# An FFT-and-experts kernel: the flag before the branch, the first rows of the redo in the branch, idle matmuls in two waits, and scatters without an order

## The chip, the cores and the metric

The kernel runs on one core of a Trainium2 chip. The metric is the device time of one execution in microseconds (us). The engines are named as in the profile: PE is TensorE, with PEld its weight loads, DVE is VectorE, ACT is ScalarE, POOL is GpSimd and SP is SyncE. A q behind an engine's name (PEldq, SPq, POOLq) is its sequencer: loads of a register, branches, waits and DMA issues.

## What is computed

Three layers stand one behind the other, on 8 sequences of 3072 tokens with 256 channels (24576 tokens): a spectral mixing, a first expert layer of hidden width 2048 that all tokens share, and a second layer of 8 experts with 768 places each, of which a token uses one.

```python
    X = np.fft.rfft(x, axis=1)
    Xr, Xi = (X.real.astype(np.float32), X.imag.astype(np.float32))
    Yr = Xr @ w_r - Xi @ w_i + b_r
    Yi = Xr @ w_i + Xi @ w_r + b_i
    lam = 0.01
    Yr = np.sign(Yr) * np.maximum(np.abs(Yr) - lam, 0.0)
    Yi = np.sign(Yi) * np.maximum(np.abs(Yi) - lam, 0.0)
    Y = Yr.astype(np.float64) + 1j * Yi.astype(np.float64)
    y = np.fft.irfft(Y, n=x.shape[1], axis=1)
...
    h = np.maximum(x @ w_in, 0.0)
    return (h * h @ w_out).astype(np.float32)
...
    logits = x @ w_gate
    expert_idx = np.argmax(logits, axis=1)
...
    for i in range(N):
        e = expert_idx[i]
        if counts[e] < capacity:
            disp[e, counts[e]] = x[i]
            pos[i] = counts[e]
            counts[e] += 1
            keep[i] = True
    h = np.maximum(np.einsum('ecd,edf->ecf', disp, w1), 0.0)
    y = np.einsum('ecf,efd->ecd', h, w2)
    out = np.zeros((N, D), dtype=np.float32)
    for i in range(N):
        if keep[i]:
            out[i] = gate_w[i] * y[expert_idx[i], pos[i]]
```

The 8 experts have 6144 places for 24576 tokens. Once all places are taken, no later token changes the output.

## The kernel before

**Main loop.** The tokens are worked in 48 blocks of 512 (NBLK, BLK), six to a sequence (BPB). The hidden width of the first expert layer is cut into 16 f steps (KF). In each f step `l1` makes one piece of the hidden layer, and steps of the spectral stage of a later sequence (`mix_a`, `mix_b`, `sa` and others, one after the other from a list) run in between. The last step of `mix_b` ends in four additions on POOL (L362, the tile y).

Blocks 0 to 10 are full: `l2` makes their output rows, which are scattered to `disp`, the experts' places. All later blocks are late: only the logits of the gate are made (`l2_gate`, bf16, into acc[0]), and the input rows of those tokens that got a place are scattered to a list `late` in DRAM, for the output to be made afterwards (redo). `route` holds the routing of a block as a list of small operations, of which the loop runs up to five in each f step of the next block: the prefix sums of the counts (`places`, giving pos), ok, kf and kp (which tokens stay), the place numbers, cnt (the counts so far), the ranks in the late list (`ranks`, lp, lx, li), the scatter to `late` in four parts (up to MV = 4 per f step), then mn (the smallest count), flag (1 if any expert has room), lcnt and nlate (the length of the list).

From block 12 on (NSURE), each late block has a check at f step 9 (FX): what is left of the routing is run, one spectral step if one is halfway, and all engines load flag (L1132) and go on only if it is 1 (L1133). The nest of conditions is closed behind the loop (L1165): an engine that finds 0 branches to the end, and there waits for what the others and the DMA queues still have open. The loop was left at the 20th check, in block 31.

**Redo.** Behind the loop, four last gate matmuls run (acc[0], L580). Then all engines load nlate (L1216), SP loads the first 256 rows of `late` (`redo_load`, into a tile of the ring zt) and the first expert's weights (`m2_loadw`), TensorE transposes the rows (`redo_y`, L1210), and chunks of 256 rows follow, each under a condition on nlate: `l1` and, three steps behind, `l2` (L565, matmuls of WO = 264 columns: 256 channels and 8 logits, of which the redo does not use the logits). Six chunks run. Their rows are scattered to `disp`.

**Second expert layer.** For each of 8 experts: the rows of `disp` are loaded (zd, L1262), transposed (L1294), and multiplied (L1327, L1351, both f32r) in six tiles of 128 rows. DVE writes yo (L1360) and POOL scatters it to the output rows of its tokens (L1361), 48 scatters in all. Each of them waits for the one before to land, since both write to `out`.

What sets the order: the order in which the program is written is each engine's queue, and the tile framework puts in the waits between engines and DMA queues.

Of the kernel before, what the change touches and what calls it, by code (L numbers as in the profile page):

```python
# [8 lines left out]
F32 = mybir.dt.float32  # L9
# [18 lines left out]
def fft_mix__moe__moe2_kernel(  # L28
# [40 lines left out]
    FX = 9  # L69
# [21 lines left out]
    PER_F = 5  # L91
    assert 3 * E <= CG and KF % 4 == 0
# [467 lines left out]
    def l2(acc, f, q, tiles=TPB):  # L560
        sh, sl = q[f]
        for t in range(tiles):
            n = 0
            for a, m in ((sh, 0), (sh, 1), (sl, 0)):
                nc.tensor.matmul(  # L565
                    acc[t][:, 0:WO],
                    a[:, t * P:(t + 1) * P],
                    wo_s[:, m, f, :],
                    start=(f == 0 and n == 0),
                    stop=(f == KF - 1 and n == 2),  # L570
                )
                n += 1
# [92 lines left out]
    def route(i, zt, lg, lt):  # L665
# [53 lines left out]
        if lt is not None:  # L719
            kf = small([TPB], F32, "kf")  # L720
            op(v.tensor_reduce, kf, ok, axis=AX.X, op=ALU.add)
            op(v.tensor_copy, kp5[:, 0:TPB], kf)
        op(v.tensor_tensor, u, pos[:, 0:TPB, :], be(ebase), op=ALU.add)
# [3 lines left out]
        op(v.tensor_copy, cnt, pos[:, TPB, :])  # L727
        last = [
            lambda: v.tensor_reduce(mn, cnt, axis=AX.X, op=ALU.min),
            lambda: v.tensor_scalar(flag, mn, float(cap), None, op0=ALU.is_lt),  # L730
        ]
        if lt is not None:
# [8 lines left out]
            ops += [None, ranks]  # L741
# [64 lines left out]
    def setup_c():  # L806
# [17 lines left out]
        nc.gpsimd.iota(tid, pattern=[[P, TPB]], base=0, channel_multiplier=1)  # L824

# [96 lines left out]
    with tc.manual_schedule():  # L922
# [120 lines left out]
        W.li = Ring("li", [P, TPB], I32, 2, lb)  # L1043
        wk_es = ExitStack()
# [16 lines left out]
        cond = ExitStack()  # L1061
        for i in range(NBLK):
# [21 lines left out]
            for f in range(KF):  # L1084
# [40 lines left out]
                if f == FX and i >= NSURE:  # L1125
                    while moves or rops:
                        step = (moves or rops).pop(0)
                        if step is not None:
                            step()
                    if pair[0]:  # L1130
                        fft(1)
                    rv = nc.values_load(flag[0:1, 0:1], min_val=0, max_val=1)  # L1132
                    cond.enter_context(tc.If(rv > 0))  # L1133
# [19 lines left out]
        cond.enter_context(tc.If(rv > 0))  # L1153
# [11 lines left out]
        cond.close()  # L1165
# [20 lines left out]
        if NBLK > NFULL:  # L1186
# [7 lines left out]
            def redo_load(c):  # L1194
                rows = W.zt()
                nc.sync.dma_start(
                    out=rows[:, 0:RT, :],
                    in_=late[c * RB:(c + 1) * RB, :].rearrange("(t p) d -> p t d", p=P),
                )
                return rows  # L1200
# [14 lines left out]

            nv = nc.values_load(nlate[0:1, 0:1], min_val=0, max_val=NREDO * RB)  # L1216
            nxt = redo_load(0)
            w_t[0] = m2_loadw(0)
            y_nxt = redo_y(nxt)
            for c in range(NREDO):  # L1220
                cond.enter_context(tc.If(nv > c * RB))
                rows, y = nxt, y_nxt
                q = []
                for f in range(KF):
# [6 lines left out]
                    if f >= RLAG:  # L1231
                        l2(acc, f - RLAG, q, RT)
                for f in range(KF - RLAG, KF):
                    l2(acc, f, q, RT)
                evac_z(acc, rows, RT)
                scatter(disp, NSLOT, lambda t: rows[:, t, D + 2:D + 3], rows, tiles=RT)
            cond.close()
# [66 lines left out]
        w_t[1] = m2_loadw(1)  # L1304
        for step in m2_split(0, nc.vector) + m2_tr(0):
            step()
        for e in range(E):
# [37 lines left out]
            for t in range(CT):  # L1345
# [15 lines left out]
                nc.gpsimd.indirect_dma_start(  # L1361
# [8 lines left out]
                )  # L1370
# [70 lines left out]
```

## Time and profile before

| what | us |
|---|---|
| median of 3 runs | 2146.16 (2144.68 to 2149.83) |
| span of the profiled execution, first to last instruction | 2143.0 |
| TensorE busy in it | 2058.0 (96%) |
| DVE, ACT, POOL busy | 1389.7, 1121.7, 763.8 |
| leaving the loop, last gate matmul to first transpose of the redo | 1675.4 to 1688.5 |
| redo to first transpose of the second expert layer | 1832.5 to 1842.6 |
| last tile of the output to the end | 2129.7 to 2143.0 |

The profile is of one execution; its time beside the span is not listed, and the span lies 3.2 us below the median. Times of a row count from the span's start. In a timeline a row is: start, duration, engine, line, operation, output <- inputs, shape, count, and in brackets the idle time of that engine before it and what ended it. The columns of a view by source line are engine, operation, inputs and count, then the shortest, median and longest duration in ns, then the first and last start in us.

### The profile page before, as it was taken

How to read it: one execution, taken by the hardware profiler on the slowest of the kernel's cores; microseconds unless marked ns; L12 is line 12 of the kernel's file. 1: busy time of each engine (PE TensorE's matmuls, PEld its weight loads, DVE VectorE, ACT ScalarE, POOL GpSimd, SP SyncE). 2: the span in 40 equal slices, each digit the busy share in tenths (PEclk: the TensorE clock that was granted, in tenths of full speed). 3: DMA queues.
4: the chain of work that ended last, by engine and by line, in shares of the span. 5: the costliest groups of instructions: out<-in, count | busy, mean ns of one | idle time of the engine just before them, and what ended most of it. 6: DMA issues, size and time to landing. Idle time of an engine off the chain costs nothing. (4 is left out here: it accounts for less than half of the span.)

```text
span 2143.0 us, 35810 instructions
## 1 busy us (share of the span) xinstructions
PE 2058.0 (96%) x13307; PEld 1756.3 (82%) x13307; DVE 1389.7 (65%) x2814; ACT 1121.7 (52%) x2227; POOL 763.8 (36%) x728
## 2 busy tenths in 40 slices
PE   6899999999999999999999999999999799799997
PEld 3878999989999987777677776777777699799997
DVE  3855666644666665888868886688858566434332
ACT  4644444454454445666656666566656455433331
POOL 2641222110222222566426554365625210244441
PEclk8978999999999999999999999999999899899999
DMA  9758665134111115221242213411152100523300
GB/s 272 227 172 302 197 211 178 55 104 119 50 43 46 41 43 157 61 60 57 84 128 58 61 37 114 121 52 56 39 159 73 58 27 25 172 93 116 97 21 25
DMA packets 163080, 214.89 MB, mean 100 GB/s; under 512 B 14622, under 2 KB 136020, under 8 KB 162882
## 3 DMA queue, kind: packets, MB, share of 16 engines
q1 hardware_dynamic: 145538, 167.94, 26.4%
q0 software_dynamic: 10848, 21.63, 3.1%
q10 hardware_dynamic: 6496, 22.81, 3.1%
q8 instruction: 109, 1.79, 0.4%
q14 instruction: 89, 0.73, 0.1%
HBM read 117.95 MB, written 104.43 MB: 104 GB/s over the span
## 5 line engine op out<-in xcount | busy, mean ns | idle before, releaser
L528 PE MATMUL ph<-yh,wi_s 128*128 128x512 f32 (+1 forms) x1780 | 512.2, 410 | 3.9 <-ACT yh L514 2.8
L362 POOL TENSOR_TENSOR y<-tt,cc 64x256 f32<-64x256 f32 x256 | 247.3, 966 | 503.1 <-DVE cc L357 421.8
L528 PEld LDWEIGHTS ph<-yh,wi_s 128*128 128x128 f32 x1780 | 309.1, 189 | 95.4 <-issue 43.3
L565 PE MATMUL acc<-wo_s,sh 128*128 128x264 f32 x1792 | 339.4, 286 | 0.0
L556 DVE TENSOR_TENSOR s<-s 128x512 f32<-128x512 f32 (+1 forms) x272 | 168.5, 619 | 230.6 <-ACT sh L555 230.5
L565 PEld LDWEIGHTS acc<-wo_s,sh 128*128 128x128 f32 x1792 | 287.0, 188 | 13.9 <-issue 1.0
L545 POOL TENSOR_TENSOR ld<-ld 128x512 bf16<-128x512 f32 x164 | 179.5, 1098 | 320.6 <-DVE ld L544 210.9
L544 DVE TENSOR_TENSOR ld<-ls 128x512 f32<-128x512 f32 x329 | 261.2, 798 | 46.4 <-ACT ls L541 44.0
L528 PE MATMUL ph<-yl,wi_s 128*128 128x512 f32 (+1 forms) x890 | 270.7, 385 | 0.2
L565 PE MATMUL acc<-wo_s,sl 128*128 128x264 f32 x896 | 254.7, 284 | 0.2 <-DVE sl L557 0.2
L552 ACT ACTIVATE s<-ph 128x512 f32<-128x512 f32 (+1 forms) x224 | 123.1, 550 | 247.5 <-PE ph L528 246.9
L541 ACT ACTIVATE ls<-ls 128x512 f32<-128x512 f32 x330 | 208.6, 632 | 10.4
L540 ACT ACTIVATE ls<-ph 128x512 f32<-128x512 f32 x221 | 131.3, 594 | 152.2 <-PE ph L528 148.8
L528 PEld LDWEIGHTS ph<-yl,wi_s 128*128 128x128 f32 x890 | 163.2, 189 | 35.1 <-DVE yl L517 1.5
L557 DVE TENSOR_TENSOR sl<-s,sh 128x512 fp32r<-128x512 f32 (+1 forms) x272 | 173.4, 638 | 19.9 <-PE px L247 0.5
L565 PEld LDWEIGHTS acc<-wo_s,sl 128*128 128x128 f32 x896 | 168.5, 188 | 0.5 <-DVE sl L557 0.4
L528 PE MATMUL acc<-yh,wi_s 128*128 128x512 f32 (+1 forms) x628 | 164.7, 384 | 0.5 <-ACT yh L514 0.4
L555 ACT ACTIVATE sh<-s 128x512 fp32r<-128x512 f32 (+1 forms) x272 | 151.4, 557 | 8.6
L545 DVE TENSOR_TENSOR ld<-ld 128x512 bf16<-128x512 f32 x165 | 149.5, 906 | 5.7
L1336 ACT ACTIVATE rh<-pg 128x384 fp32r<-128x384 f32 x128 | 62.7, 490 | 168.0 <-PE pg L1327 166.4
L1351 PE MATMUL po<-w2s,rh 128*128 128x256 f32 x768 | 139.1, 284 | 0.0
L1327 PE MATMUL pg<-xh,w1s 128*128 128x384 f32 x512 | 138.3, 342 | 0.0
(290 smaller groups left out, 3820.4 us busy)
## 6 DMA issues: line engine op xcount, KB each, us to landing
out_dram<-zero SPq DMA_DIRECT2D x48, 512.0 KB, 4.8
u<-ue ACTq DMA_DIRECT2D x53, 384.0 KB, 4.2
uj<-u SPq DMA_DIRECT2D x77, 256.0 KB, 4.0
z<-zj SPq DMA_DIRECT2D x74, 256.0 KB, 2.2
xc<-in_x_dram SPq DMA_DIRECT2D x48, 384.0 KB, 5.3
xc<-z SPq DMA_DIRECT2D x48, 384.0 KB, 3.8
m<-table SPq DMA_DIRECT2D x77, 128.0 KB, 3.1
ma<-table SPq DMA_DIRECT2D x77, 128.0 KB, 4.0
```

The lines of the kernel that those rows point to most:

```text
L362: y_eng[n == r].tensor_tensor(y[64 * r:64 * r + 64, :], t[src, r, :], c[src, r, :], op=ALU.subtract)
L528: nc.tensor.matmul(p, wi_s[:, l, k, f * P:(f + 1) * P], y[:, k, 0:n_tok], start=(n == 0), stop=(n == 5),)
L540: nc.scalar.activation(s, p, AF.Relu)
L541: nc.scalar.activation(s, s, AF.Square)
L544: nc.vector.tensor_tensor(d, s, top(s), op=ALU.subtract)
L545: (gp if f in E_POOL else ve).tensor_tensor(e, d, top(d), op=ALU.subtract)
L555: nc.scalar.activation(sh, s, AF.Square)
L556: nc.vector.tensor_tensor(s, s, s, op=ALU.mult)
L557: nc.vector.tensor_tensor(sl, s, sh.bitcast(F32), op=ALU.subtract)
L565: nc.tensor.matmul(acc[t][:, 0:WO], a[:, t * P:(t + 1) * P], wo_s[:, m, f, :], start=(f == 0 and n == 0), stop=(f == KF - 1 and n == 2),)
L1327: nc.tensor.matmul(p[:, 0:gs], w1s[:, l, k, f * P:(f + 1) * P], y[:, k, g * gs:(g + 1) * gs], start=(n == 0), stop=(n == 5),)
L1351: nc.tensor.matmul(acc, a[:, t * P:(t + 1) * P], w2s[:, m, f, :], start=(n == 0), stop=(n == 3 * KD - 1),)
```

## The change

- The flag is made right behind kf and kp, ahead of the place numbers, and the check stands at f step 8 and not at 9. The break between two f steps ahead of `ranks` is gone, and lcnt and nlate are now the last of the list.
- Each condition gets an else branch (`leave`): there TensorE runs 16 matmuls (WARM) of the identity with 256 columns of zeros into acc[3], which nobody reads, and SP loads the first 256 rows of `late` into a tile of their own (row0). The same load stands at the end of the innermost condition. Behind the join, the first rows are transposed ahead of the load of nlate and of the weights.
- The redo's `l2` is 256 columns wide.
- Behind the redo, TensorE runs 16 such matmuls again.
- All output scatters are declared to be free of an order among themselves (a token has one place at most).

```diff
-    FX = 9
+    FX = 8
+    WARM = 16
...
-    def l2(acc, f, q, tiles=TPB):
+    def l2(acc, f, q, tiles=TPB, width=WO):
...
-                    acc[t][:, 0:WO],
+                    acc[t][:, 0:width],
                     a[:, t * P:(t + 1) * P],
-                    wo_s[:, m, f, :],
+                    wo_s[:, m, f, 0:width],
...
             op(v.tensor_copy, kp5[:, 0:TPB], kf)
+        op(v.tensor_copy, cnt, pos[:, TPB, :])
+        op(v.tensor_reduce, mn, cnt, axis=AX.X, op=ALU.min)
+        op(v.tensor_scalar, flag, mn, float(cap), None, op0=ALU.is_lt)
         op(v.tensor_tensor, u, pos[:, 0:TPB, :], be(ebase), op=ALU.add)
...
-        op(v.tensor_copy, cnt, pos[:, TPB, :])
-        last = [
-            lambda: v.tensor_reduce(mn, cnt, axis=AX.X, op=ALU.min),
-            lambda: v.tensor_scalar(flag, mn, float(cap), None, op0=ALU.is_lt),
-        ]
+        last = []
...
-            ops += [None, ranks]
+            ops.append(ranks)
...
+    def late_rows(c, rows):
+        nc.sync.dma_start(
+            out=rows[:, 0:RB // P, :],
+            in_=late[c * RB:(c + 1) * RB, :].rearrange("(t p) d -> p t d", p=P),
+        )
...
+        row0 = lb.tile([P, RB // P, DW], F32, name="row0")
...
-        cond = ExitStack()
+        ifs = []
+
+        def go_on(value):
+            guard = tc.If(value)
+            ifs.append((guard, guard.__enter__()))
+
+        def warm(p):
+            for _ in range(WARM):
+                nc.tensor.matmul(p[:, 0:D], idt, zero)
+
+        def close_ifs(other=None):
+            while ifs:
+                guard, here = ifs.pop()
+                guard.__exit__(None, None, None)
+                if other:
+                    with here.Else():
+                        other()
+
+        def leave():
+            warm(acc[3])
+            late_rows(0, row0)
...
-        cond.close()
+        late_rows(0, row0)
+        close_ifs(leave)
         if carry:
             l2_gate(acc, KF - 4, carry, first=8)
...
+            nxt = row0
+            y_nxt = redo_y(nxt)
             nv = nc.values_load(nlate[0:1, 0:1], min_val=0, max_val=NREDO * RB)
-            nxt = redo_load(0)
             w_t[0] = m2_loadw(0)
-            y_nxt = redo_y(nxt)
             for c in range(NREDO):
...
-                        l2(acc, f - RLAG, q, RT)
+                        l2(acc, f - RLAG, q, RT, D)
                 for f in range(KF - RLAG, KF):
-                    l2(acc, f, q, RT)
+                    l2(acc, f, q, RT, D)
...
-            cond.close()
+            close_ifs()
+            warm(acc[3])
...
+        sent = []
...
-                nc.gpsimd.indirect_dma_start(
+                inst = nc.gpsimd.indirect_dma_start(
...
-                )
+                ).ins
+                for prev in sent:
+                    tc.declare_no_dep(inst, prev, reason="every token has one slot at most")
+                sent.append(inst)
```

What stands in the engines' queues shows two places. A number behind a name (ld_8208) tells one buffer from another; what an instruction waits for stands in brackets (DMASW and DMAHW are lanes of DMA queues).

First, DVE in the routing of block 30, which runs in block 31 ahead of the 20th check. Before, from cnt to nlate:

```order
L671 COPY cnt<-pos 128x8
L544 TENSOR_TENSOR ld_8208<-ls_8202 128x512 [waits PE_49,Activation_49]
L545 TENSOR_TENSOR ld_8208<-ld_8208 128x512 [waits DVE_49]
L739 TENSOR_SCALAR lp<-acc_1537,lcnt 128x5 [waits PE_49]
L671 SCALAR_TENSOR_TENSOR lx<-lp,kp_91 128x4 [waits DVE_49]
L671 TENSOR_SCALAR li_1551<-lx 128x4 [waits DVE_49]
L729 TENSOR_REDUCE mn<-cnt 128x1
L544 TENSOR_TENSOR ld_8209<-ls_8203 128x512 [waits Activation_49,Pool_49]
L545 TENSOR_TENSOR ld_8209<-ld_8209 128x512 [waits DVE_49]
L730 TENSOR_SCALAR flag<-mn 128x1 [waits DVE_sequencer_49,PE_sequencer_49,SP_sequencer_49,Activation_sequencer_49,Pool_sequencer_49]
L747 COPY lcnt<-lp 128x1
L748 CAST nlate<-lp 128x1
```

And after, from pos on:

```order
L706 TENSOR_TENSOR pos<-px,cnt 128x40 [waits PE_49]
L672 SCALAR_TENSOR_TENSOR ok<-pos,oh_90 128x32 [waits DVE_49]
L672 TENSOR_REDUCE kf<-ok 128x4 [waits DVE_49]
L672 CAST kp_91<-kf 128x4 [waits DVE_49]
L672 COPY cnt<-pos 128x8
L545 TENSOR_TENSOR ld_8208<-ls_8202 128x512 [waits Activation_49]
L672 TENSOR_REDUCE mn<-cnt 128x1 [waits DVE_49]
L672 TENSOR_SCALAR flag<-mn 128x1 [waits PE_sequencer_49,DVE_sequencer_49,Activation_sequencer_49,SP_sequencer_49,Pool_sequencer_49,DVE_49]
L672 TENSOR_TENSOR rv<-pos,ebase 128x32
L672 TENSOR_TENSOR rv<-rv,ok 128x32 [waits DVE_49]
L672 TENSOR_REDUCE sf<-rv 128x4 [waits DVE_49]
L545 TENSOR_TENSOR ld_8209<-ls_8203 128x512 [waits PE_49,Activation_49]
```

The three operations on cnt, mn and flag now stand right behind kp, ahead of rv (the place numbers) and of lp, lx and li (the ranks), which follow further down.

Second, the way out of the loop. SP's queue before, from the join on:

```order
L1216 TENSOR_LOAD nlate [waits DVE_49]
L1216 ISA x2
L1196 DMA zt_1546<-late 128x2x259 [waits DMASW6_49,DMASW5_49,DMASW7_49,DMASW1_49,DMAHW0_49,DVE_49,Activation_49]
L1181 DMA yT<-in_moe_w_dram 128x2x1024 [waits DMAHW1_49,PE_49]
L1182 DMA yT<-in_moe_w_dram 128x8x256 [waits DMAHW2_49,PE_49,Activation_49]
L1237 COMPARE_AND_BRANCH
```

After, with one of the else branches (up to its UNCONDITIONAL_BRANCH) and then the join:

```order
L827 DMA row_1552<-late 128x2x259 [waits DMAHW6_49,DMASW5_49]
L1081 UNCONDITIONAL_BRANCH [waits SP_sequencer_49,DMAHW0_49,DMAHW1_49,DMAHW2_49,DMAHW3_49,DMAHW4_49,DMAHW5_49,DMAHW7_49]
L1244 TENSOR_LOAD nlate [waits DVE_49]
L1244 ISA x2
L1210 DMA yT<-in_moe_w_dram 128x2x1024 [waits DVE_49,DMAHW1_49,PE_49,Activation_49]
L1211 DMA yT<-in_moe_w_dram 128x8x256 [waits DVE_49,DMAHW2_49,PE_49,Activation_49]
L1081 COMPARE_AND_BRANCH
```

The load of the first rows stands in the branch and waits for two lanes; before, it stood behind the join and behind the load of nlate and waited for seven sources.

TensorE's queue at the same place before, from the last gate matmul on:

```order
L580 LDWEIGHTS wgate
L580 MATMUL acc_1535<-ld_8209,wgate 32x512
L1216 TENSOR_LOAD nlate [waits DVE_49]
L1210 MATMUL px<-idt,zt_1546 128x128 [waits DMAHW0_49,DVE_49,PE_49]
L1210 MATMUL px<-idt,zt_1546 128x128
L1210 MATMUL px<-idt,zt_1546 128x128 [waits DVE_49,PE_49]
L1210 MATMUL px<-idt,zt_1546 128x128
L1237 COMPARE_AND_BRANCH
```

And after, behind the join and the first of the four gate matmuls (the 16 added matmuls stand in the else branches, each of which ends in a jump to the join):

```order
L581 LDWEIGHTS wgate
L581 MATMUL acc_1535<-ls_8204,wgate 32x512 [waits Activation_49]
L581 LDWEIGHTS wgate
L581 MATMUL acc_1535<-ld_8210,wgate 32x512
L581 LDWEIGHTS wgate
L581 MATMUL acc_1535<-ld_8210,wgate 32x512
L1236 MATMUL px<-idt,row_1552 128x128 [waits DMAHW4_49,DMAHW2_49,DMAHW5_49,DMAHW1_49,DMAHW6_49,DMAHW0_49,DMAHW7_49,DVE_49,PE_49]
L1236 MATMUL px<-idt,row_1552 128x128
L1236 MATMUL px<-idt,row_1552 128x128 [waits DVE_49,PE_49]
L1236 MATMUL px<-idt,row_1552 128x128
L1244 TENSOR_LOAD nlate [waits DVE_49]
L1081 COMPARE_AND_BRANCH
```

The transposes (L1236) now stand ahead of the load of nlate, and read row0 (row_1552).

## Rows read from the trace of the kernel before

**Rows 1.** The profiled page, busy time of each engine, share of the span, instructions.

```profile
PE 2058.0 (96%) x13307; PEld 1756.3 (82%) x13307; DVE 1389.7 (65%) x2814; ACT 1121.7 (52%) x2227; POOL 763.8 (36%) x728
```

**Rows 2.** Busy time by stage, first row its columns.

```profile
core 0: us, PE busy (x) PEld busy (x) DVE busy (x) ACT busy (x) POOL busy (x), PEclk, DMA share, GB/s
...
1675.40:1688.50 13.10, 0.62 (x4) 0.21 (x4) 1.53 (x4) 0.00 (x0) 5.27 (x7) 0.68 0.18 46
1688.50:1693.80 5.30, 5.16 (x22) 4.71 (x23) 1.74 (x5) 2.36 (x6) 0.00 (x0) 0.50 1.05 380
1693.80:1832.50 138.70, 138.65 (x1160) 138.44 (x1158) 85.43 (x208) 79.24 (x206) 9.96 (x10) 1.00 0.07 22
1832.50:1842.60 10.10, 0.00 (x1) 0.03 (x1) 5.05 (x5) 3.91 (x5) 1.94 (x2) 0.73 0.38 120
1842.60:1850.80 8.20, 7.47 (x26) 6.67 (x27) 2.79 (x5) 2.74 (x6) 0.00 (x0) 0.50 1.03 364
```

**Rows 3.** Timeline of TensorE, leaving the loop.

```profile
1684.00 0.59 PE L580 MATMUL acc<-ld,wgate 128*32 128x512 bf16 x1 [8.69 <-POOLq L1165]
...
1688.53 1.08 PE L1210 MATMUL px<-idt,zt 128*128 128x128 f32 x4 [3.92 <-DMA zt<-late]
```

**Rows 4.** Timeline of SP's queue, the same place.

```profile
1685.58 0.38 SPq L1196 DMA_DIRECT2D zt<-late  x1
```

**Rows 5.** Timeline of POOL, the same place.

```profile
1677.42 0.97 POOL L647 DMA_INDIRECT late<-zt,li  x1 [0.30 <-DMA late<-zt,li]
...
1680.92 1.50 POOL L362 TENSOR_TENSOR y<-tt,cc 64x256 f32<-64x256 f32 x2 [1.00 <-issue]
```

**Rows 6.** Instructions of L1165, the end of the loop; durations in ns.

```profile
L1165 PEldq COMPARE_BRANCH  x21: 65/65/3497, 877.7 to 1678.0; - x21
...
L1165 POOLq INC_SWDGE_SEM  x1: 931/931/931, 1684.5 to 1684.5; - x1
```

**Rows 7.** Timelines at the end of the program, DVE first, then POOL.

```profile
2115.29 0.48 DVE L1360 TENSOR_SCALAR yo<-po,zd 128x256 f32<-128x256 f32 x1 [1.79 <-PE po L1351]
...
2129.69 0.48 DVE L1360 TENSOR_SCALAR yo<-po,zd 128x256 f32<-128x256 f32 x1 [2.39 <-PE po L1351]
...
2116.05 0.97 POOL L1361 DMA_INDIRECT out_dram<-yo,zd  x1 [17.00 <-DVE yo L1360]
...
2133.18 0.97 POOL L1361 DMA_INDIRECT out_dram<-yo,zd  x1 [2.21 <-DMA out_dram<-yo,zd]
```

**Rows 8.** Timeline of DVE, flag before the last check.

```profile
1673.49 0.15 DVE L730 TENSOR_SCALAR flag<-mn 128x1 int32<-128x1 f32 x1
```

**Rows 9.** Instructions of L1132, the check's load of flag; durations in ns.

```profile
L1132 PEldq TENSOR_LOAD <-flag x20: 298/303/821, 877.1 to 1673.7; - x20
```

**Rows 10.** Timeline of TensorE, inside the redo.

```profile
1780.40 0.64 PE L528 MATMUL acc<-yh,wi_s 128*128 128x256 f32 x4
...
1781.11 0.40 PE L565 MATMUL acc<-wo_s,sh 128*128 128x264 f32 x2
...
1781.47 0.40 PE L565 MATMUL acc<-wo_s,sh 128*128 128x264 f32 x2
```

**Rows 11.** Waits of TensorE while checks run, 877 to 1660 us.

```profile
PE acc L580 <- DVE flag L730: 0.8, 3, 0.4
```

**Rows 12.** Plain f32 matmuls of 256 columns, timeline, then L371's instructions.

```profile
1666.49 0.59 PE L371 MATMUL px<-y,ma 128*128 128x256 f32 x2
...
L371 PE MATMUL px<-y,ma x186: 377/379/483, 50.1 to 1666.7; 128*128 128x256 f32 x186
```

**Rows 13.** Instructions of L1237, the end of the redo; durations in ns.

```profile
L1237 POOLq COMPARE_BRANCH  x8: 34/34/50, 1686.7 to 1838.2; - x8
...
L1237 PEldq COMPARE_BRANCH  x8: 65/65/4086, 1688.7 to 1835.8; - x8
```

**Rows 14.** Timeline of TensorE, first matmuls of the second expert layer.

```profile
1842.60 1.94 PE L1294 MATMUL pt<-idt,zd 128*128 128x128 f32 x8 [10.14 <-DMA zd<-disp]
...
1846.29 0.67 PE L1327 MATMUL pg<-xh,w1s 128*128 128x384 f32 x1
```

More of the change, by code (lines that the diff above doesn't have):

```diff
@@ L1132, in fft_mix__moe__moe2_kernel @@
                     rv = nc.values_load(flag[0:1, 0:1], min_val=0, max_val=1)
-                    cond.enter_context(tc.If(rv > 0))
+                    go_on(rv > 0)
                 if i < NSURE:
@@ L1152, in fft_mix__moe__moe2_kernel @@
         rv = nc.values_load(flag[0:1, 0:1], min_val=0, max_val=1)
-        cond.enter_context(tc.If(rv > 0))
+        go_on(rv > 0)
         if carry:
@@ L1195, in redo_load @@
                 rows = W.zt()
-                nc.sync.dma_start(
-                    out=rows[:, 0:RT, :],
-                    in_=late[c * RB:(c + 1) * RB, :].rearrange("(t p) d -> p t d", p=P),
-                )
+                late_rows(c, rows)
                 return rows
@@ L1214, in redo_y @@
                 return yh, yl
+            nxt = row0
+            y_nxt = redo_y(nxt)
             nv = nc.values_load(nlate[0:1, 0:1], min_val=0, max_val=NREDO * RB)
-            nxt = redo_load(0)
             w_t[0] = m2_loadw(0)
-            y_nxt = redo_y(nxt)
             for c in range(NREDO):
-                cond.enter_context(tc.If(nv > c * RB))
+                go_on(nv > c * RB)
                 rows, y = nxt, y_nxt
@@ L1369, in fft_mix__moe__moe2_kernel @@
                     oob_is_err=False,
-                )
+                ).ins
+                for prev in sent:
+                    tc.declare_no_dep(inst, prev, reason="every token has one slot at most")
+                sent.append(inst)
 def _tables():
```

## The prediction

> **What bounds the kernel now.** I read the busy shares first, then the stages, then what ends each long idle time of TensorE. TensorE is busy for 2058.0 of 2143.0 us [rows 1], so work taken off another engine is worth nothing unless TensorE waits for it. The table by stage [rows 2] shows where TensorE does not run: 13.1 us between leaving the loop and the first redo matmul (0.62 us busy), and 10.1 us between the redo and the second expert layer (none); a third gap lies at the end, told below. Behind each of the two stands a short stretch with the granted clock at 0.50, which is 1.2 GHz: 5.3 us and 8.2 us. The change works on these three gaps, on the check that comes before them, and on the width of one matmul.
>
> First gap. TensorE waits 8.69 us for POOL's part of the branch, runs four gate matmuls from 1684.00, then waits 3.92 us for the redo rows and starts transposing at 1688.53 [rows 3]. The rows come late because SP issues their load at 1685.58, 2.95 us before the transposes [rows 4]. SP's load stands behind the join, and what it waits for is POOL: POOL is busy with the y steps of the spectral stage until 1682.42 [rows 5] and ends its part of the branch with an instruction of 0.931 us that starts at 1684.5 [rows 6].
>
> End. An output scatter takes 0.97 us on POOL and the next starts 2.21 us later, when it has landed: 3.18 us from one to the next, while the tiles come faster, since the queue of scatters is late at the end. The last tile is ready at 2129.69 + 0.48 = 2130.17 and its scatter starts at 2133.18, 3.01 us late; one that waited for its tile alone started 0.28 us behind it (2115.29 + 0.48, then 2116.05) [rows 7].
>
> **The change part by part, against the profiled span of 2143.0 us.** The median of the three runs is 2146.16, 3.2 us above it; I take the same shift for the median.
>
> 1. *Leaving the loop.* The first load goes into a tile of its own, in the branch, behind the landing of the last late scatter and not behind the join. That scatter starts at 1677.42 and has landed by about 1680.9, when POOL's second pair of y steps goes on at 1680.92 [rows 5]. Landed rows are then to be had at about 1681 + 2.95 = 1684. TensorE stays bound by POOL: its spectral steps are still ahead of the check in POOL's queue, with the same landing before the second pair, so POOL is no earlier. I put it later by 0.3 us for two DVE operations of 0.15 us that now stand ahead of the late list [rows 8], and by as much again, an estimate, for the spectral step that has moved ahead of it. The gates start at 1684.0 + 0.6 = 1684.6, take 0.4, and the transposes follow at 1685.0: 1688.53 - 1685.0 = **-3.5**. Bounds: 0 if a load still ends last as now; -5.7 if nothing but the landing counted; -2.5 to -4.7 when POOL's time alone is unsure. The load of nlate, now behind the transposes, lies beside the splits. The weight loads of the first expert follow it on SP; their first reader stands behind the redo.
> TensorE's branch that leaves took 3.497 us where one that stays takes 0.065 [rows 6]. The last one began at about 1674.2, behind the load. It now comes one f step earlier; the twenty loads lie (1673.7 - 877.1)/19 = 41.9 us apart [rows 9], 2.6 us per f step. TensorE is then in its else branch at about 1675.1, and 16 matmuls there end by 1678.5 to 1682.0 (step 5 has their price), before POOL. The Trainium skill ("Runtime: NRT & Kernel Launch", section "Instruction fetch mechanics") states that a taken branch whose target is not in the window held forces a fetch; the trace agrees for the way in (3.497 us). By that rule the jump out of the longer else code could cost as much again; with the matmuls at half clock TensorE would be out at 1685.5, and this term would be -2.6 instead of -3.5.
>
> 2. *End.* With no order between scatters the last one starts 0.28 us behind its tile, at 2130.45 and not at 2133.18, and what follows it stays: **-2.7**. Bounds: -3.0 (no start cost at all) and 0 (still in order).
>
> 3. *Redo width.* Six chunks run; 16 f steps, two tiles, three matmuls: 576 matmuls of 256 instead of 264 columns. Start to start, 256 columns take (1781.11 - 1780.40)/6 = 118 ns and 264 columns (1781.47 - 1781.11)/3 = 120 ns [rows 10]. TensorE is the bound there (138.65 of 138.70 us busy [rows 2]). At 2 ns: **-1.2**; bounds -0.6 (1 ns) and -1.9 (8 columns at 2.4 GHz, 3.3 ns).
>
> 4. *The checks.* Twenty checks run (blocks 12 to 31). Before, flag is written late (1673.49, and the loads read it at 1673.7 [rows 8, 9]); TensorE's sequencer waits for it in its own load, 298 ns at the least and 821 at most [rows 9]. The trace shows 0.8 us of TensorE idle on flag in three checks [rows 11]; a part of the load's 0.298 us may show in others. The new flag is written two f steps ahead of the check. What is queued behind the load is the next l1 and the gate matmuls that used to stand ahead; TensorE's queue keeps matmuls for it as now. **-1.0**; bounds -2 (the 0.8 and four more loads) and +2 (0.1 us lost per check through the gate matmuls that move behind it).
>
> 5. *Second gap.* Sixteen f32 matmuls of 256 columns now go ahead of the transposes of the expert layer. Two plain f32 matmuls of that size take 0.59 us from the first start to the last end where one takes 0.38 [rows 12], so 0.21 from start to start: 3.4 us at 2.4 GHz, 6.9 at 1.2. TensorE is out of the redo at about 1836 (its last branch starts at 1835.8) and is held to 1838.3 at the latest, if by POOL's last branch of 1838.2 [rows 13]. They end between 1839.5 and 1845.2; the rows for the transposes land at 1842.6 [rows 14]. Up to there they are hidden; behind it they cost up to +2.6. What they can give: the f32 matmuls from 1846.29 to 1850.80 ran at half clock [rows 2, 14], worth half of 4.5, 2.25, and 0.5 in the transposes, of which most is waiting for splits. Between -2.7 and +2.6 I take **-1.0**: in most of the outcomes they end before 1842.6, and only a part of the stretch gets the higher clock.
>
> 6. *Clock behind the first gap.* The 16 matmuls in the branch are over at about 1679 to 1682 and TensorE then does nothing again until 1684.6. Before, the clock was granted at 0.68 on the mean over the gap of 13.1 us and at 0.50 behind it [rows 2]. I take **0**; bounds -2.6 (half of the 5.3 us) and +1.5 (they delay the gates).
>
> Sum: -3.5 - 2.7 - 1.2 - 1.0 - 1.0 + 0 = -9.4, with 2146.16 some **2136.8 us**.
>
> **The rivals.** *A: the clock stays at 2.4 GHz through both gaps.* For it: both sets of matmuls are there for that, and at 1693.80 and 1850.80 the clock had come up a few microseconds into steady work. Against: idle time still follows each of them. Steps 6 and 5 become -2.6 and -2.7, the sum -13.7: 2132.5.
>
> *B: the matmuls of the second gap run at half clock and late, and the clock is low again when the expert layer starts.* Step 5 becomes +2.6, the sum -5.8: 2140.4. For it: in the gap the granted clock was 0.73 on the mean and 0.50 right behind [rows 2], and the transposes that began at 1842.60 ran their whole time at 0.50. The Trainium skill ("TensorE: Matmul & The Clock Gate", section "Part 4: PE-mode transpose") states that transposes do not count as activity for the higher clock; the trace agrees as far as it goes (0.50 until 1850.80, with matmuls only from 1846.29).
>
> *C, slower: the check stalls TensorE.* The load of the flag now stands ahead of the gate matmuls of f = 9, so the matmuls that hid a load's time could be missing. Price c per check, twenty times. The other steps give -8.4; from c = 0.42 us all is lost, from 0.74 us the kernel is slower by over 0.3%. At 1.0 (the longest load, 0.82, a branch of 0.065 and 0.1 to refill) it is 2157.8. Against: the load and the branch now take 0.30 + 0.065, twenty of them cost about 0.8 us in all on flag, and the flag comes earlier.
>
> *D: the scatters still go in order* (the wait stays in some other form, say by POOL's own queue). Step 2 is 0: 2139.5. Against: nothing but the landing of the one before ends their idle time [rows 7].
>
> **How the numbers follow.** The forecast has a chance of 0.62, A 0.15, B 0.14, C 0.05, D 0.04. A measurement of this kernel can tell about 0.3%, 6.4 us, from no change: the bound is at 2139.8. Of the forecast 0.06 lies above it, all of B and half of D. So faster by over 0.3% 0.73, within 0.3% 0.22, slower by over 0.3% 0.05. The forecast alone, with step 1 between -4.7 and -2.5, steps 3 and 4 within their bounds and step 5 between its ends, is 2133 to 2141; A and B with their own bounds lie from 2130.5 to 2143, which holds eight in ten with C left out.
>
> **What would show it.** Step 1: the load of the first rows starts before 1682 by the clock of before, and the transposes wait for POOL, not for a DMA. Step 2: the last scatters start 0.3 us behind their tiles. Step 3: 16 f steps of the redo shorter by some 0.2 us a chunk (96 matmuls of 2 ns). Step 4: no idle time of TensorE on flag. Steps 5 and 6: the granted clock at the first l1 of the redo and at the first matmul of the expert layer, and whether the added matmuls end before the rows land. Wrong would make it: idle time of TensorE at each of the twenty checks (C), a POOL branch that is much later than 1685, or added matmuls that end last in either gap.

## The result, and the profile after

The changed kernel takes 2168.64 us (median of 4 runs, 2164.46 to 2174.08), the kernel before 2145.83: a ratio of 1.0108, 95% interval 1.0095 to 1.0120. It is slower by 23 us where 9 us less were forecast, and lies outside the forecast range. The profiled execution is the longest of the four (span 2172.4, 2174.08 in all); an execution takes 1.7 us more than its span.

Stage by stage, from the timelines of the two profiled executions and of the best version that the experiments led to (its run is told below), in us. Left out are 1.2 us of splits ahead of the redo and 9.8 us behind the last scatter's start, the same in all three:

| stage | before | after | best |
|---|---|---|---|
| TensorE's first load of flag, from the start | 877.1 | 876.2 | 877.6 |
| first to twentieth load of flag | 796.6 | 830.2 | 796.2 |
| from there to the first transpose of the redo | 14.9 | 15.7 | 11.1 |
| first `l1` of the redo to its last matmul | 142.7 | 141.5 | 140.6 |
| from there to the expert layer's first matmul on weights | 13.8 | 14.5 | 14.1 |
| from there to the last tile yo | 283.9 | 282.9 | 284.0 |
| last tile to the start of its scatter | 3.0 | 0.3 | 0.3 |
| span | 2143.0 | 2172.4 | 2134.9 |

One stage holds the loss: the twenty blocks with checks, 33.6 us longer. The check's loads of flag, as [rows 9] for before (durations in ns, first and last start in us):

```profile
L1160 PEldq TENSOR_LOAD <-flag x20: 301/305/595, 876.2 to 1706.4; - x20
```

The longest load is shorter than before (595 ns against 821), and no row of TensorE's waits in the loop names flag any more. What it waits for instead (us in total, times, longest), in the stretch 878 to 1660:

```profile
PE acc L581 <- DVE ld L546: 5.3, 12, 0.7
PE acc L323 <- ACT s L454: 5.1, 3, 1.7
PE px L323 <- ACT s L454: 5.1, 3, 1.7
...
PE px L372 <- DVE a L266: 2.3, 2, 1.2
PE px L323 <- DVE s L455: 2.0, 3, 0.7
PE acc L323 <- DVE s L455: 2.0, 3, 0.7
```

L323 are the matmuls of `mix_a` and `mix_b`; s is their input, which ACT and DVE split in two from what the transform `s2` (L248) left. Six waits of 1.7 us on ACT, and six of 0.7 on DVE. The place, at the end of block 12, in TensorE's timeline (start, duration, line, in brackets the idle time and what ended it):

```profile
895.88 0.60 PE L248 MATMUL acc<-m,uj 128*128 128x128 f32 x4
896.32 1.03 PE L372 MATMUL px<-y,ma 128*128 128x256 f32 x4
899.05 0.50 PE L323 MATMUL acc<-wmix,s 128*128 128x256 f32 x2 [1.71 <-ACT s L454]
900.24 0.74 PE L323 MATMUL acc<-wmix,s 128*128 128x256 f32 x4 [0.68 <-DVE s L455]
```

And the same step in the kernel before:

```profile
892.92 1.03 PE L371 MATMUL px<-y,ma 128*128 128x256 f32 x4
893.60 1.28 PE L528 MATMUL acc<-yh,wi_s 128*128 128x512 f32 x4
...
895.21 1.25 PE L322 MATMUL acc<-wmix,s 128*128 128x256 f32 x6
```

Before, an `l1` of some 1.6 us (L528) stands between the two `sa` matmuls (L371) and `mix_a` (L322), and the split is done behind it. After, `mix_a` follows at once, and TensorE stands idle for 1.71 + 0.68 us. This happens in seven of the twenty blocks (from 897, 1023, 1158, 1285, 1421, 1547 and 1683 us), 16.7 us in all. Behind five of them the granted clock falls to 0.50; the five stretches are 17 us together, so about 8.5 us more are lost (an estimate: half of them). That is some 25 of the 33.6 us. The busy time by 1 us behind the second of the seven (PE, PEld, DVE, ACT, POOL, then PEclk):

```profile
1023.00:1024.00 1.00, 0.00 (x0) 0.00 (x0) 0.88 (x3) 0.56 (x2) 0.99 (x1) 1.00 0.00 0
1024.00:1025.00 1.00, 0.47 (x2) 0.30 (x2) 1.00 (x3) 0.94 (x3) 1.00 (x2) 1.00 0.00 0
...
1026.00:1027.00 1.00, 1.00 (x6) 1.00 (x6) 0.00 (x0) 0.00 (x0) 0.00 (x0) 0.50 0.77 262
...
1029.00:1030.00 1.00, 1.00 (x7) 0.88 (x6) 0.97 (x3) 0.13 (x1) 0.00 (x0) 1.00 0.03 8
```

What the three gaps became, first the stages as in [rows 2] (leaving the loop, start of the redo, redo to transposes, transposes):

```profile
1709.40:1721.50 12.10, 7.15 (x32) 6.09 (x33) 2.61 (x7) 0.53 (x1) 7.27 (x8) 1.00 0.13 34
1723.30:1728.30 5.00, 4.98 (x22) 4.89 (x23) 2.50 (x6) 2.48 (x7) 0.00 (x0) 0.50 0.97 358
...
1864.90:1876.50 11.60, 8.74 (x33) 7.36 (x34) 5.06 (x5) 3.93 (x5) 1.94 (x2) 0.85 0.36 112
1876.50:1879.30 2.80, 1.60 (x13) 1.13 (x12) 1.29 (x2) 1.39 (x3) 0.00 (x0) 1.00 0.97 336
```

The added matmuls run at a granted clock of 1.00 in the first gap, and it is 0.50 again behind it all the same. In the second it is 0.85, and 1.00 behind it. The end, as in [rows 7], DVE's last tile:

```profile
2161.77 0.48 DVE L1388 TENSOR_SCALAR yo<-po,zd 128x256 f32<-128x256 f32 x1 [2.39 <-PE po L1379]
```

And POOL's last scatter, 0.28 us behind it:

```profile
2162.53 0.97 POOL L1389 DMA_INDIRECT out_dram<-yo,zd  x1 [1.91 <-DVE yo L1388]
```

### The profile page after: what moved, and what is told of

The parts are those of the page before. It is cut to its first block, busy times and chain, and to the rows that moved or that the text cites. A ratio compares the mean times of both kernels' runs of the same rounds, so it can differ in the third digit from the quotient of the medians.

```text
span 2172.4 us, 35927 instructions
## 1 busy us (share of the span) xinstructions
PE 2079.5 (96%) x13349; PEld 1768.5 (81%) x13349; DVE 1391.9 (64%) x2812; ACT 1120.5 (52%) x2224; POOL 762.2 (35%) x728
## 5 line engine op out<-in xcount | busy, mean ns | idle before, releaser
L363 POOL TENSOR_TENSOR y<-tt,cc 64x256 f32<-64x256 f32 x256 | 240.4, 939 | 494.5 <-DVE cc L358 388.9
L566 PE MATMUL acc<-wo_s,sh 128*128 128x264 f32 (+1 forms) x1792 | 338.8, 285 | 0.0
L566 PEld LDWEIGHTS acc<-wo_s,sh 128*128 128x128 f32 x1792 | 286.9, 188 | 14.1 <-issue 1.0
L545 DVE TENSOR_TENSOR ld<-ls 128x512 f32<-128x512 f32 x328 | 255.5, 780 | 45.7 <-ACT ls L542 39.0
L566 PE MATMUL acc<-wo_s,sl 128*128 128x264 f32 (+1 forms) x896 | 254.1, 284 | 0.2 <-DVE sl L558 0.2
L546 DVE TENSOR_TENSOR ld<-ld 128x512 bf16<-128x512 f32 x164 | 141.5, 863 | 5.7
```

The source lines that it names most:

```text
L363: y_eng[n == r].tensor_tensor(y[64 * r:64 * r + 64, :], t[src, r, :], c[src, r, :], op=ALU.subtract)
L545: nc.vector.tensor_tensor(d, s, top(s), op=ALU.subtract)
L546: (gp if f in E_POOL else ve).tensor_tensor(e, d, top(d), op=ALU.subtract)
L566: nc.tensor.matmul(acc[t][:, 0:width], a[:, t * P:(t + 1) * P], wo_s[:, m, f, 0:width], start=(f == 0 and n == 0), stop=(f == KF - 1 and n ...
```

## The experiments

The medians of before were 2145.5 to 2147.2 us in these sessions; each ratio is against the runs of before beside it.

### The spectral steps, the check and the routing's order

The idle time of `mix_a` has three possible sources: (A) the line that takes one spectral step more when a pair is half done at the check (`if pair[0]: fft(1)`), (B) the check one f step earlier, (C) the new order of the routing. A follows from counting: 16 steps belong to each block, 13 in the f steps and 3 at the block's end, and the pattern (s2, s2, sa, sa, mix_a, mix_b) has six. At f step 9 eight steps of the block are done, and no pair was ever half done; at f step 8 seven are done, so that the first block of each sequence takes one more. From there on all steps stand one place ahead, and the three at the end of the first and fourth block are sa, sa, mix_a and not s2, sa, sa.

**after_paid** gives the step back at the block's end.

```diff
             q = []
+            owed = 0
...
                     if pair[0]:
                         fft(1)
+                        owed = 1
...
-            fft(len(SKIP[full]))
+            fft(len(SKIP[full]) - owed)
```

> The changed kernel, with the one extra spectral step that a check at f step 8 takes in the first and fourth block of a sequence paid back at that block's end (two steps there and not three), so that the steps at block ends are those of the kernel before. Theory A (the extra step shifts the list of spectral steps, so that in seven blocks mix_a stands right behind the transform it needs, 2.4 us idle each, and TensorE's clock falls behind five of these idle times): the loop takes 797 us again from first to last check, 2139 to 2144 us in all. Theory B (the check one f step earlier stalls the engines at each check, 1.7 us each): stays at 2164 to 2172. Theory C (the order of the routing, with flag ahead of the ranks, delays DVE): stays at 2164 to 2172.

Measured 2147.44 us (ratio 1.0010, 1.0000 to 1.0019): 21 us of the 23 are gone, though not down to the 2139 to 2144 of A. The loop takes 804.5 us from first to last load and not the 797 of A. One reason is that `mix_a` still waits for s at the same seven places, though only 0.3 and 0.7 us and with no fall of the clock (878 to 1660 us):

```profile
PE px L323 <- DVE s L455: 2.1, 3, 0.8
PE acc L323 <- DVE s L455: 2.1, 3, 0.7
PE px L323 <- ACT s L454: 1.9, 6, 0.3
...
PE acc L323 <- ACT s L454: 1.2, 4, 0.3
```

These rows are 7.3 us, before 0.9. The same waits stand in before_fx8_paid below, which has the old order of the routing, and not in after_fx9: they come with the early check, although its extra step is paid back.

**after_fx9** puts the check back.

```diff
-    FX = 8
+    FX = 9
```

> The changed kernel with the check at f step 9 again; all else as changed. Theory A (shifted spectral steps): no pair is open at f step 9, no extra step is taken, 2138 to 2143 us. Theory B (the early check stalls): also 2138 to 2143. Theory C (the routing's order): stays at 2164 to 2172.

Measured 2151.57 us (1.0028, 1.0017 to 1.0039). 17 us are gone, and 5.6 are left in the loop (802.2 us from first to last load): none of the three expected that number, and C is true for a part.

**before_bunch** makes the bad neighbours in the kernel before.

```diff
-                if f not in SKIP[full] or o == BPB - 1:
+                off = SKIP[full]
+                if i >= NSURE and o in (0, 3):
+                    off = (2, 5)
+                if i >= NSURE and o in (1, 4):
+                    off = (1, 2, 5, 10)
+                if f not in off or o == BPB - 1:
```

> The kernel before, with nothing changed but one spectral step: in the first and fourth late block of a sequence one step more is taken (at f step 10), in the block behind it one less (at f step 1). In seven blocks that run, mix_a then stands right behind the transform it needs, as in the changed kernel. Theory A: 7 times 2.4 us, and up to 1.7 us more for each fall of the clock: 2160 to 2175 us. Theories B and C: 2146, as before.

Measured 2165.3 us (1.0093, 1.0076 to 1.0110), 20 us more, with one spectral step moved in seven blocks and nothing else changed. At the end of block 12 its timeline has the same idle times as the changed kernel:

```profile
894.03 1.03 PE L371 MATMUL px<-y,ma 128*128 128x256 f32 x4
896.76 0.50 PE L322 MATMUL acc<-wmix,s 128*128 128x256 f32 x2 [1.71 <-ACT s L453]
897.97 0.73 PE L322 MATMUL acc<-wmix,s 128*128 128x256 f32 x4 [0.71 <-DVE s L454]
```

All seven places have the 1.71 us, and behind it 0.7 us (four) or 0.3 (three). In the profiled execution, the fastest of four at 2160.75 us, the granted clock stays at 1.00 behind all seven, and the loop takes 811.5 us, 14.9 more than before.

**before_fx8_paid** is the early check by itself, with flag as late as before (`FX = 8` and the lines of after_paid).

> The kernel before with the check at f step 8 and not at 9, and the extra spectral step paid back at the block's end. Theory A: 2143 to 2149 us, no change. Theory B (the early check stalls, here with the flag made late as well): 2165 or more. Theory C: no change.

Measured 2211.99 us (1.0307, 1.0284 to 1.0331). Here TensorE does stall at the check, as the first waits show (878 to 1735 us; nlate is the last operation of the routing):

```profile
PE ph L528 <- DVE nlate L748: 17.7, 6, 4.5
PE acc L528 <- DVE nlate L748: 10.8, 4, 4.4
```

So at f step 8 the routing of before is not done in time, and the early flag is what makes that check possible at all: with it the same place costs no such wait.

**before_route** is the new order of the routing alone, in the kernel before: cnt, mn and flag behind kp, and `ops.append(ranks)`.

> The kernel before with the new order of the routing alone (cnt, mn, flag right behind kp, no break ahead of the ranks), check at f step 9. Theory D: 2151 to 2152 us. Theory E: 2146, as before.

Measured 2151.44 us (1.0029, 1.0019 to 1.0038): 5.2 us. One of TensorE's waits (876 to 1680 us):

```profile
PE acc L580 <- POOL ld L545: 8.1, 6, 1.6
```

The same row of before (876 to 1674):

```profile
PE acc L580 <- POOL ld L545: 3.4, 6, 0.6
```

4.7 us of the 5.2 are in these six waits, 0.7 to 1.0 us more in each of six blocks, of the gate matmuls on a piece of the gate that POOL makes. POOL's queue tells why, in the same block of both; in before_route:

```profile
915.75 1.44 POOL L647 DMA_INDIRECT late<-zt,li  x1 [3.23 <-DVE ld L544]
...
922.05 3.89 POOL L362 TENSOR_TENSOR y<-tt,cc 64x256 f32<-64x256 f32 x4
926.01 1.30 POOL L545 TENSOR_TENSOR ld<-ld 128x512 bf16<-128x512 f32 x1
```

And in before:

```profile
916.65 1.50 POOL L647 DMA_INDIRECT late<-zt,li  x1 [2.76 <-DVE ld L544]
...
922.36 4.23 POOL L362 TENSOR_TENSOR y<-tt,cc 64x256 f32<-64x256 f32 x4
926.66 1.04 POOL L545 TENSOR_TENSOR ld<-ld 128x512 bf16<-128x512 f32 x1
```

TensorE runs 1.36 us earlier in the first (it reaches these gate matmuls at 925.16 and not at 926.52), but POOL's scatters to `late` start only 0.90 earlier, the additions of y behind them 0.31, and the piece of the gate behind those is done at 927.31 and not at 927.70. mn and flag stand ahead of li, li holds the scatters, the scatters hold the additions, these the gate: TensorE waits 1.57 us and not 0.60. li is done 4.32 us behind kp and not 3.87; the rest of the delay comes on POOL, whose four scatters take 5.36 us here and 4.76 before, for a reason that no row shows.

**route_flag** and **route_none** are its halves: the three operations moved with the break kept, and the break taken out alone.

> The kernel before with cnt, mn and flag moved right behind kp; the break ahead of the ranks stays. The new order of the routing as a whole cost 5 to 6 us. Theory D1 (it is the three operations ahead of the place numbers, behind which the next operation on pos takes 1.06 us and not 0.18): 2150 to 2152 us. Theory D2 (it is the missing break): 2146, as before.

> The kernel before without the break ahead of the ranks; cnt, mn and flag stay where they were. Theory D1: 2146 us. Theory D2: 2150 to 2152.

Measured 2162.06 (1.0065, 1.0040 to 1.0090) and 2158.58 (1.0054, 1.0035 to 1.0072): each half costs more than both together, which neither theory had. TensorE's waits in route_flag (878 to 1660 us):

```profile
PE acc L580 <- POOL ld L545: 13.1, 6, 2.3
```

And in route_none:

```profile
PE acc L632 <- DVE kp L671: 7.5, 7, 1.7
PE px L632 <- DVE kp L671: 4.4, 5, 1.7
```

With five operations to an f step, two more ahead push the ranks behind the break into the next f step, and the scatters, the additions and the gate follow (13.1 us of waits on POOL). Without the break they come one f step too early, and TensorE reaches the ranks' matmul (L632) before kp is made (11.9 us). In the new order as a whole the two nearly cancel: in seventeen of the twenty blocks of before_route li is done 0.4 to 0.5 us later behind kp than before, in three 0.1.

### The idle matmuls

**old_route** is the changed kernel with FX = 9 and the routing of before; **old_route_nowarm2** takes out the 16 matmuls behind the redo as well, and **old_route_nowarm** those in the branch too.

```diff
         def leave():
-            warm(acc[3])
             late_rows(0, row0)
...
             close_ifs()
-            warm(acc[3])
```

> The changed kernel with the check at f step 9 and with the routing in the order of before (place numbers, ranks, then mn and flag); first rows, both sets of idle matmuls, width and scatters as changed. Theory D (the new order of the routing delays DVE's pieces of the gate, 0.3 us for each block): the loop from first to last check falls from 802.2 to about 797 us, 2146 us in all. Theory E (the 5.6 us come from the branch that now has an else part, or from the new tile): stays at 2151.

> The kernel of the run old_route without the 16 idle matmuls behind the redo. Theory F (these matmuls run past the landing of the expert's rows, 5 us, and give back 2 us of clock): 3 us less than old_route, about 2143. Theory G (they pay for themselves through the higher clock): the same as old_route or 2 us more.

> The kernel of the run old_route_nowarm2 without the 16 idle matmuls of the branch either. If these keep TensorE's clock at 2.4 GHz at the start of the redo, as the trace of after_fx9 has it: 2 us more than old_route_nowarm2, about 2145. If they only stand in TensorE's way: 1 us less.

Measured 2144.81 (0.9991, 0.9981 to 1.0000), 2142.43 (0.9981, 0.9971 to 0.9991) and 2138.79 us (0.9964, 0.9949 to 0.9979). The loop is back at 796 to 797 us. Both sets cost time here by the medians: 2.4 us behind the redo, where the two intervals overlap, and 3.6 in the branch where the opposite was expected. TensorE leaving the loop, with both sets:

```profile
1677.91 7.14 PE L1077 MATMUL acc<-zero,idt 128*128 128x256 f32 x32 [2.80 <-ACTq L1082]
1685.83 0.40 PE L581 MATMUL acc<-ld,wgate 128*32 128x512 bf16 x1 [0.78 <-issue]
```

Without the second set:

```profile
1678.18 10.11 PE L1077 MATMUL acc<-zero,idt 128*128 128x256 f32 x32 [2.80 <-ACTq L1082]
1690.55 0.40 PE L581 MATMUL acc<-ld,wgate 128*32 128x512 bf16 x1 [2.25 <-issue]
```

Without any:

```profile
1682.66 0.59 PE L581 MATMUL acc<-ld,wgate 128*32 128x512 bf16 x1 [9.10 <-POOLq L1082]
...
1683.21 1.12 PE L1236 MATMUL px<-idt,row 128*128 128x128 f32 x4
```

The 16 matmuls are 32 records and take 7.14 us, at a granted clock of 1.00; in the second kernel the granted clock is 0.50 for their first 6 us and they take 10.11. The two kernels are the same up to the redo's end; from the last load of flag to the first transpose it is 12.8 us in one and 17.2 in the other. Behind them TensorE needs 0.78 and 2.25 us more until the gate matmuls start, and these wait for no other engine. TensorE's queue shows what they wait for, its own jump out of the else branch, in old_route (durations in ns):

```profile
L1082 PEldq COMPARE_BRANCH  x29: 65/65/4592, 877.3 to 1832.3; - x29
```

The longest of these 29 branches lasts 4.59 us from 1681.2, and the one in old_route_nowarm2 6.07 us from 1684.4; a part is hidden behind the matmuls still in the queue. It comes on top of one of 3.3 to 3.9 us at the way in that all kernels have. All five kernels with matmuls in the else branch have such a second branch ahead of the redo, of 3.3 to 6.1 us, and none of the others has. Without the matmuls TensorE waits for POOL alone and goes on at 1682.66. The extra wait for the jump is in line with the Trainium skill ("Runtime: NRT & Kernel Launch", section "Instruction fetch mechanics"), by which a jump out of what is held must fetch; these rows don't show the fetch itself.

In old_route the granted clock stays at 1.00 through this gap and into the redo, as the matmuls were meant to do, and still nothing is won, since TensorE stands once more a few us into the redo, this time with nothing that the profile shows to wait for (after_fx9 has the same, 2.47 us):

```profile
1691.47 0.74 PE L529 MATMUL acc<-yh,wi_s 128*128 128x256 f32 x4 [2.37 <-issue]
```

The redo takes 142.2 us in old_route, and 141.0 in old_route_nowarm, where the clock is 0.50 at its start.

TensorE behind the redo, in old_route with the matmuls:

```profile
1835.58 9.53 PE L1077 MATMUL acc<-zero,idt 128*128 128x256 f32 x32 [6.19 <-ACT w1s L454]
1844.94 1.04 PE L1322 MATMUL pt<-idt,zd 128*128 128x128 f32 x8
...
1847.81 0.42 PE L1356 MATMUL pg<-xh,w1s 128*128 128x384 f32 x1
```

9.53 us from 1835.58, 6.2 us behind the redo's end, and the transposes start only when they are over; they then run at a clock of 1.00 and the expert layer to its last tile takes 281.8 us where it takes 284.1 without. 2.3 us are gained, 4.1 lost (18.4 us from the redo's end to the first matmul on weights, against 14.3). In the changed kernel's profiled execution the same matmuls start 2.9 us behind the redo, and it is about even: 14.5 us and not 13.8, then 282.9 and not 283.9.

**after_nowarm** is the changed kernel without both.

> The changed kernel without both sets of idle matmuls. By the runs so far they cost 6 us (2.4 behind the redo, 3.6 in the branch): 2162 to 2164 us where the changed kernel takes 2168.6. If they are worth something where the clock happens to be high, as in the profile of the changed kernel: 2168 or more.

Measured 2171.13 us (1.0108, 1.0087 to 1.0128), no gain: in the changed kernel the late list is itself late in the last block, POOL comes out at 1721.5, and the matmuls in the branch are over before. Its TensorE there:

```profile
1710.65 7.15 PE L1076 MATMUL acc<-zero,idt 128*128 128x256 f32 x32 [1.31 <-DVE ld L545]
1721.55 0.59 PE L581 MATMUL acc<-ld,wgate 128*32 128x512 bf16 x1 [3.76 <-POOLq L1081]
```

What they cost depends on what else is late.

### What is left

**paid_nowarm** puts the causes together: after_paid without both sets.

> The changed kernel with the extra spectral step paid back and without both sets of idle matmuls. Left are the check at f step 8 and the new order of the routing. If the causes add up: 2147.4 less 2 to 6 for the matmuls, 2141 to 2145 us. If the early check costs by itself as well: 2147 or more. If the idle matmuls are free in this kernel, as in after_nowarm: 2147.

Measured 2143.60 us (0.9981, 0.9969 to 0.9994), within the 2141 to 2145 for causes that add up. Strictly they don't: without both sets it is 3.8 us less here, 6.0 in old_route and nothing in the changed kernel. It stays 5.5 us above best_again below, and not for the routing's order alone. Its loop takes 805.0 us; `mix_a` waits 7.0 us for s as in after_paid, the gate 5.1 for POOL where it was 3.4 before, and at the way out the first transposes wait 4.44 us for the DMA of the first rows.

**best8** tries the early check with the routing of before and only mn and flag moved, ahead of the break.

> The best version so far (routing in the order of before, first rows in the branch, width, scatters, no idle matmuls) with the check at f step 8, mn and flag right behind cnt and ahead of the break, and the extra spectral step paid back. If the flag is there in time, the way out comes one f step earlier, up to 2.3 us less than 2138.8: 2136 to 2139. If the check waits for flag: 2142 or more.

Measured 2150.65 us (1.0017, 1.0008 to 1.0027): in the loop 814 us and not 796, so the early check is not to be had in this way either.

**best_again** is old_route_nowarm once more, with more executions.

> The version of old_route_nowarm again (first rows in the branch, width, scatters; check at f step 9, routing in the old order, no idle matmuls), in more rounds: 2137 to 2141 us, 0.995 to 0.998 of before, by the first gap -3.5, the end -2.7 and the redo -1.2.

Measured 2138.11 us (0.9957, 0.9943 to 0.9970), faster than both kernels: the change without the early check, the new routing order and the idle matmuls. TensorE at its way out of the loop:

```profile
1684.31 0.58 PE L581 MATMUL acc<-ld,wgate 128*32 128x512 bf16 x1 [8.93 <-POOLq L1082]
...
1684.86 1.11 PE L1236 MATMUL px<-idt,row 128*128 128x128 f32 x4
```

And SP:

```profile
1680.63 0.37 SPq L828 DMA_DIRECT2D row<-late  x1
```

SP's load of the first rows is issued at 1680.63, 4 us ahead of the transposes, which now wait for POOL alone; before, it was issued behind POOL [rows 3, 4].

## Why the prediction was wrong

**Step 4, the checks: wrong, and it holds the whole loss.** The step priced the earlier check by the flag's stalls (-1.0) and, as its worst case, by the gate matmuls that then stand behind it (+2). It put the spectral steps that move with the check at nothing. The stalls went away as forecast, though flag is written 1.0 to 3.3 us ahead of the load and not two f steps. But 33.6 us came in the loop. The larger cause was in the diff's one number: FX also decides whether `if pair[0]: fft(1)` runs, and so where all later spectral steps stand. Step 1 speaks of "the spectral step that has moved ahead" in the block that leaves and never asks what it does in the nineteen others: 21 us by the medians (after_paid, and before_bunch from the other side), 25.7 in the loop of the profiled executions. The smaller one stood in the prediction, at the wrong place: step 1 put the late list 0.3 us later and priced it once, at leaving. It is 0.4 to 0.5 us later in most blocks, POOL's queue makes more of it, and in six blocks TensorE waits for that: 5.2 us (before_route). That is the price of the order in the kernel before. In the changed kernel's own waits no row names POOL, and what after_paid leaves of the loop's loss, 7.9 us, is for the larger part `mix_a`'s waits; how much of the 33.6 is the order's is not shown.

**Rival C** has the sign and the order of size (2157.8 forecast, 2168.6 measured), but not the mechanism: no idle time on flag, and the loop loses its time at block ends and at a gate matmul some f steps behind the check. It is what happens to before_fx8_paid, at some 3.3 us for each check.

**Step 1, leaving the loop.** The mechanism is right: in best_again the transposes come 11.1 us behind the last load of flag, before 14.9, which is the -3.5 of the forecast and 0.3 more. In the changed kernel it didn't show (15.7), since the scatters to `late` start 3.4 us behind the load of flag (1709.83 and 1706.38) and before 0.8 ahead of it: the check moved up one f step, the late list didn't. The jump out of the else code does cost as much again as the way in, as the step allowed; in the changed kernel its 3.65 us are over before POOL comes out.

**Step 2, the end: right**, 2.73 us in the changed kernel as forecast (0.28 us from tile to scatter, before 3.01).

**Step 3, the width: about right.** The redo takes 140.4 to 142.2 us in the profiled executions of the ten kernels with 256 columns (141.1 on the mean) and 142.0 to 143.0 in the six with 264 (142.4): 1.4 us less, where 1.2 were forecast. The two ranges touch, since other things differ at the redo's start; the two longest of the ten are old_route and after_fx9, with their idle times of 2.37 and 2.47 us.

**Steps 5 and 6, the idle matmuls: mis-sized.** [rows 12] is one record, and a plain f32 matmul leaves two (x32 for 16 matmuls): 7.1 us at 2.4 GHz where the step took 3.4. With that price, and when they start late or run in part at half clock, they end behind the rows of the expert layer: in old_route by 4.1 us, in the changed kernel by less than one. What they can give back was sized right (2.3 us in the expert layer of old_route), and in the branch they gave nothing back that the times show.

**Rivals A, B and D.** In the changed kernel's profiled execution the clock was at 0.50 behind the first gap, against A, and at 1.00 behind the second, against B; the matmuls of the second gap ended late, as B has it, but by less than one us. D is out by step 2.

Taken together, without step 4's causes and the idle matmuls the rest of the sum (-3.5, -2.7, -1.2) is -7.4, 2138.8 us; best_again is at 2138.1, 9.0 us below the runs of before beside it (2147.15).

## What to carry to other kernels

A number that places a check or a wait may also feed a condition in the code around it: before the moved thing is priced, count what the condition does in all rounds and compare the neighbours in each engine's queue over a whole period, not only at the place of the change. A delay of half a microsecond on a small operation is priced by the longest chain behind it, in every round where an engine waits for the end of that chain (here six of twenty). Idle matmuls that hold the clock are to be priced by their records at the lower clock, against what the wait has left.

## What the runs showed of the hardware

Two idle times of 1.71 and 0.68 us with half a microsecond of matmuls between them were followed by a granted clock of 0.50 in five places of seven of the changed kernel, and in none of the four such places of before_bunch; in route_flag one idle time of 2.1 to 2.3 us was, in five places of six, and in old_route two of 2.80 and 2.37 us were not. The length of an idle time alone does not tell here whether the clock falls. In the second gap of the changed kernel the clock stayed at 1.00 through 2.8 us of transposes behind the idle matmuls. The Trainium skill ("TensorE: Matmul & The Clock Gate", section "Part 4: PE-mode transpose") states that transposes don't count as activity for the higher clock; no run here shows it fall in so short a stretch of them.
